# Constant matrices made by GpSimd instead of VectorE, and a newly searched order, in an attention and feed-forward kernel

## The chip, the cores and the metric

The kernel runs on one core of one Trainium2 chip. The metric is the device time of that core in microseconds, the median over the runs given. The core has a matrix engine (TensorE, PE in the profile; its weight loads are PEld), VectorE (DVE), ScalarE (ACT), GpSimd (POOL), and SyncE (SP), which here only issues transfers. Each engine works through its own list of instructions strictly in order, and waits at an instruction until the semaphores that it names have been raised.

## The reference, cut to what matters

Attention with a decay ("forgetting") runs over 8 batches of 8 heads, with 576 positions and a head size of 64. Its output, one row of 512 numbers per token, goes through a bilinear feed-forward layer.

```
scores = (q @ k.T) / 8
cum    = cumsum(log(clip(f, 1e-4, 1)))          # per head, along the sequence
scores = scores + cum[:, None] - cum[None, :]   # then -1e9 above the diagonal
attn   = softmax(scores)
x      = attn @ v                               # (4608 tokens, 512)
out    = ((x @ w_a) * (x @ w_b)) @ w_out        # 512 -> 1536 -> 512
```

## The kernel before, in words

**Work and tiles.** One batch has 8 heads, taken in pairs: pair t (0 to 31; t = 4 x batch + pair) is two heads. Two pairs make a unit u (0 to 15). The scores of a unit are made in four groups g: rows of positions 0 to 255, 256 to 383, 384 to 511, and 512 to 575. ScalarE takes the exponential ("exp0" to "exp4", by block of 128 rows), VectorE takes row maxima ("max") and reciprocals of the sums ("rec"), GpSimd multiplies by the reciprocals ("norm", line 567), and the normalized matrix is turned, on TensorE in batch 0 ("ptr", line 591, with an eviction "evp") and by transposing transfers (line 583) afterwards, so that TensorE can multiply it with v ("pv", "pve", "pv4", lines 611 to 636). The result, turned, lies in `xT` and is the input of the feed-forward layer.

The feed-forward layer runs over strips of tokens: 256 tokens from token 0, from 256 and from 512, 384 from 768, then strips of 512. For each of 12 column blocks fb, TensorE makes `psa` and `psb` (line 874, four matmuls each); one of them is copied to SBUF ("aev"), VectorE multiplies (line 890), and at the end `pso` (line 899) is made and stored. Weights `wa` and `wb` come in two pieces each: blocks fb 0 to 3 in one transfer ("the low piece", 512 KB in SBUF), blocks 4 to 11 in another ("the high piece", 1,024 KB). GpSimd's queue issues these transfers (line 365).

**Constants.** At the start, `constants` makes a 128x128 identity on GpSimd. From it VectorE makes `pick` and `eye` (reductions over blocks of the identity), `neg` (the identity times -60000), `sel` (which rows of the cumulative sum a matmul picks), `low` (ones below the diagonal, by blocks) and a row of ones `cw["1"]` for the scan. The first three batches add the decay and the mask by small matmuls with these matrices; `sel` is needed by "crep", which spreads the cumulative sum. GpSimd sets the padding (`paddings`) to zero.

**Order.** Nothing is scheduled when the kernel is built. Every step is an `op` with a number, and a table `ORDER` gives the sequence in which they are recorded; from it follows the order on each engine and the order in which buffers rotate. A second table `CHOICE` has one letter for each step that may run on more than one engine (A ScalarE, D VectorE, P GpSimd, S SyncE). Forty steps "fill" (line 178) are four matmuls each of the identity with itself, into a buffer that nobody reads: they only occupy TensorE.

## Time and profile before

| | before |
|---|---|
| runs | 401.02, 402.35, 398.56 us; median 401.02 |
| profiled execution, first to last instruction | 400.7 us |
| PE busy | 383.2 us (96%) |
| DVE busy | 315.3 us (79%) |
| ACT busy | 250.0 us (62%) |
| POOL busy | 253.6 us (63%) |
| granted TensorE clock, mean | 0.986 |

The profiled execution has only its span; no separate time is listed for it. The span is 0.3 us under the median of the three runs, and inside their spread. The page of the profile cuts the span in 40 slices of 10 us and gives for each the busy share in tenths; `PEclk` is the clock that TensorE was granted. A matmul counts as busy until its modelled end, so that a stretch in which PE is 95% busy can hold more idle time than 5%. From about 120 us on PE is busy without a gap; before that the four compute engines share the load.

### The profile page before, as it was taken

The page shows a single profiled execution, that of the slowest core. Times are in us where ns is not written, and L with a number is a line of the kernel's source. Part 1 is how long each engine was busy: PE and PEld are TensorE (multiplying, and loading weights), DVE is VectorE, ACT ScalarE, POOL GpSimd, SP SyncE. Part 2 cuts the span into 40 slices and gives each one's busy share as a digit, 9 for nine tenths or more (in the row PEclk, how much of TensorE's full clock was granted, in tenths as well). Part 3 has the DMA queues.
Part 4 walks back from the last instruction along what each step waited for, and adds up shares of the span by engine and source line. Part 5 has one row for each costly group of instructions (what it writes and reads, how often), then busy time and mean ns, then how long its engine had stood idle before and what let it go on. Part 6 is the DMA issues. An engine that isn't in the chain of part 4 may idle for free.

```text
span 400.7 us, 11076 instructions
## 1 busy us (share of the span) xinstructions
PE 383.2 (96%) x4040; PEld 212.0 (53%) x4040; DVE 315.3 (79%) x907; ACT 250.0 (62%) x757; POOL 253.6 (63%) x424
## 2 busy tenths in 40 slices
PE   8598799998999999999999999999999999999996
PEld 7466576765855544454445454544444444444553
DVE  8989798976778988997988889898969892373560
ACT  5798766666667778758785777577868673300011
POOL 3889876887397876897896849787968553000000
PEclk9889999998999999999999999999999999999999
DMA  7999989989999999999999999999997729000102
GB/s 282 240 186 289 204 177 224 213 150 215 208 301 208 227 171 330 201 277 212 295 187 286 211 255 273 233 241 190 276 187 218 157 66 202 28 2 36 71 0 79
DMA packets 148311, 78.22 MB, mean 195 GB/s; under 512 B 130592, under 2 KB 133408, under 8 KB 148256
## 3 DMA queue, kind: packets, MB, share of 16 engines
q1 hardware_dynamic: 144272, 72.53, 77.4%
q0 software_dynamic: 3696, 4.72, 7.0%
q8 instruction: 31, 0.51, 0.5%
q10 hardware_dynamic: 288, 0.26, 0.2%
q14 instruction: 24, 0.20, 0.1%
HBM read 49.69 MB, written 9.58 MB: 148 GB/s over the span
## 4 chain that ended last, share of the span: by engine, by line
PE 79%; DMA 9%; DVE 4%; POOL 2%; ACT 2%; issue 2%; SPq 0%; POOLq 0%; DVEq 0%; ACTq 0%
PE pso L899 22%; PE psa L874 22%; PE psb L874 21%; PE sc L401 8%; DMA wa<-in_moe_w_a_dram 5%; PE pv L611 2%; DVE st L488 2%; DMA k<-in_k_dram 1%; PE pv L613 1%; PE sc L636 1%; DMA PTB<-spread 1%; DMA PTB<-PB 1%; DVE qT L302 1%; PE pv L623 1%; ACT PB L550 1%
## 5 line engine op out<-in xcount | busy, mean ns | idle before, releaser
L874 PE MATMUL psa<-xT,wa 128*128 128x512 f16 (+2 forms) x528 | 116.2, 343 | 2.3 <-DMA wa<-in_moe_w_a_dram 1.7
L874 PE MATMUL psb<-xT,wb 128*128 128x512 f16 (+2 forms) x528 | 116.2, 343 | 0.1
L899 PE MATMUL pso<-wout,ht 128*128 128x512 f16 (+1 forms) x444 | 98.4, 374 | 0.0
L567 POOL TENSOR_SCALAR PA<-PA,st 128x128 f16<-128x128 f16 (+2 forms) x162 | 76.0, 482 | 31.8 <-DVE st L559 20.4
L890 DVE TENSOR_TENSOR ht<-psb,a 128x512 f16<-128x512 f32 (+2 forms) x132 | 76.2, 589 | 22.0 <-PE psb L874 15.0
L512 DVE CUSTOM_DVE_ANT_0 S<-sc,spread 128x128 f32<-128x128 f32 (+3 forms) x160 | 86.7, 567 | 7.7 <-PE sc L401 5.4
L138 ACT CAST a<-psa 128x512 f16<-128x512 f32 (+2 forms) x85 | 43.5, 515 | 55.9 <-PE psa L874 53.8
L874 PEld LDWEIGHTS <-wa 128*128 128x128 f16 x528 | 50.1, 99 | 45.5 <-issue 3.7
L874 PEld LDWEIGHTS <-wb 128*128 128x128 f16 x528 | 50.4, 99 | 41.5 <-issue 1.7
L567 POOL TENSOR_SCALAR PB<-PB,st 128x512 f16<-128x512 f16 (+1 forms) x84 | 58.7, 712 | 15.7 <-DVE st L559 14.6
L550 ACT ACTIVATE PA<-S,st 128x256 f16<-128x256 f32 (+2 forms) x120 | 59.9, 502 | 12.5 <-DVE st L512 12.4
L899 PEld LDWEIGHTS <-ht 128*128 128x128 f16 x444 | 41.7, 98 | 46.8 <-issue 1.3
L488 DVE TENSOR_REDUCE st<-sc 128x2 f32<-128x512 f32 (+7 forms) x68 | 46.3, 723 | 6.0 <-PE sc L401 5.3
L401 PE MATMUL sc<-kT,qT 32*128 32x128 f16 (+5 forms) x960 | 41.7, 272 | 5.5 <-ACT PA L550 2.1
L550 ACT ACTIVATE PB<-S,st 128x512 f16<-128x512 f32 x40 | 28.5, 714 | 7.9 <-DVE st L512 7.9
L401 PEld LDWEIGHTS <-qT 32*128 32x128 f16 (+1 forms) x960 | 18.6, 96 | 26.7 <-issue 14.4
L142 DVE CAST a<-psa 128x512 f16<-128x512 f32 (+2 forms) x47 | 26.2, 560 | 7.2 <-PE psa L874 6.6
L559 DVE RECIPROCAL st<-st 128x2 f32<-128x2 f32 x128 | 18.5, 157 | 14.0 <-ACT PA L550 8.7
L142 POOL CAST k<-k 128x1152 f16<-128x1152 f32 (+1 forms) x15 | 20.5, 1367 | 8.9 <-DMA k<-in_k_dram 8.9
L138 ACT COPY osb<-pso 128x512 f32<-128x512 f32 (+1 forms) x22 | 12.4, 570 | 19.9 <-PE pso L899 15.1
L138 ACT CAST xT<-pv 128x512 f16<-128x512 f32 (+2 forms) x39 | 17.0, 446 | 11.8 <-PE pv L636 5.8
L140 POOL TENSOR_SCALAR q<-q 128x1152 f16<-128x1152 f32 (+1 forms) x15 | 20.6, 1372 | 5.0 <-DMA q<-in_q_dram 4.2
(98 smaller groups left out, 491.5 us busy)
## 6 DMA issues: line engine op xcount, KB each, us to landing
spread<-cum_d SPq DMA_DIRECT2D x20, 576.0 KB, 5.9
out_dram<-osb SPq DMA_DIRECT2D x35, 256.0 KB, 3.8
q<-in_q_dram SPq DMA_DIRECT2D x15, 576.0 KB, 7.3
k<-in_k_dram SPq DMA_DIRECT2D x15, 576.0 KB, 5.2
v<-in_v_dram SPq DMA_DIRECT2D x32, 256.0 KB, 6.1
wout<-in_moe_w_out_dram POOLq DMA_DIRECT2D x3, 512.0 KB, 8.7
v<-in_v_dram SPq DMA_DIRECT2D x8, 128.0 KB, 7.2
wb<-in_moe_w_b_dram POOLq DMA_DIRECT2D x1, 1024.0 KB, 13.5
```

What stands on the lines that cost most here:

```text
L138: nc.scalar.copy(out=out_, in_=in_)
L140: ENG[e].tensor_scalar(out=out_, in0=in_, scalar1=0.125, scalar2=1.0, op0=MUL, op1=MUL)
L142: ENG[e].tensor_copy(out=out_, in_=in_)
L401: nc.tensor.matmul(out=dst, lhsT=lhsT, rhs=rhs, start=start, stop=stop, skip_group_check=True)
L488: nc.vector.tensor_reduce(out=m if i == 4 else st[:, 2 * i:2 * i + 2][:, h:h + 1] if isinstance(x, list) else m, in_=y, axis=AXX, op=MAX, ...
L512: nc.vector.tensor_tensor_reduce(out=o, in0=x, in1=y, scale=-1.0, scalar=3e38, op0=ADD, op1=MIN, accum_out=m)
L550: nc.scalar.activation(out=p_blocks(t, i)[:, :, h, :], in_=x.rearrange("p (j k) -> p j k", k=128), func=EXP, scale=sign, bias=st[:, c:c + ...
L559: nc.vector.reciprocal(out=st[:, 20 + 2 * i:22 + 2 * i], in_=st[:, 10 + 2 * i:12 + 2 * i])
L567: ENG[e].tensor_scalar(out=p, in0=p, scalar1=st[:, c:c + 1], scalar2=1.0, op0=MUL, op1=MUL)
L874: nc.tensor.matmul(out=o, lhsT=w16[:, db, 128 * fb:128 * fb + 128], rhs=tokens(db, t0, n), start=(db == 0), stop=(db == 3))
L890: nc.vector.tensor_tensor(out=ht[:, 0:n], in0=T.pop(("psb", t0, fb))[:, 0:n], in1=T.pop(("a16", t0, fb))[:, 0:n], op=MUL)
L899: nc.tensor.matmul(out=o, lhsT=T[("ht", t0, fb)][:, 128 * tb:128 * tb + 128], rhs=wout16[:, fb, c], start=(fb == 0), stop=(fb == 11))
```

## The change

Three things change. First, `pick`, `eye`, `neg`, `sel`, `low` and the ones are made by GpSimd. The two reductions are replaced by three additions that fold the identity (64, 32, 16 columns) through a new small tile `half`. Second, `low` keeps only its last two steps on VectorE (a scan and a subtraction); the zeros and ones of it are a GpSimd step of its own. Third, `ORDER` and `CHOICE` are other tables, found by a new search in which transfers land late at random; every engine's order differs.

```diff
+    half = fixed("half", [128, 64])
...
+    def low_blocks(_):
+        nc.gpsimd.memset(low, 0.0)
+        for a in range(1, 4):
+            nc.gpsimd.memset(low[:, a, 0:32 * a], 1.0)
+
     def lows(_):
-        nc.vector.memset(low, 0.0)
-        for a in range(1, 4):
-            nc.vector.memset(low[:, a, 0:32 * a], 1.0)
         nc.vector.tensor_tensor_scan(out=step, data0=cw["1"][:, 0:32], data1=eye, initial=0.0, op0=MUL, op1=ADD)
...
     def picks(_):
-        with nc.allow_low_precision("ones and zeros"):
-            nc.vector.tensor_reduce(out=pick, in_=ident.rearrange("p (a r) -> p r a", r=16), axis=AXX, op=ADD)
-            nc.vector.tensor_reduce(out=eye, in_=ident.rearrange("p (a n) -> p n a", n=32), axis=AXX, op=ADD)
-        nc.vector.tensor_scalar(out=neg, in0=eye, scalar1=NEGBIG, scalar2=1.0, op0=MUL, op1=MUL)
-        nc.vector.memset(sel, 0.0)
+        nc.gpsimd.tensor_tensor(out=half, in0=ident[:, 0:64], in1=ident[:, 64:128], op=ADD)
+        nc.gpsimd.tensor_tensor(out=eye, in0=half[:, 0:32], in1=half[:, 32:64], op=ADD)
+        nc.gpsimd.tensor_tensor(out=pick, in0=eye[:, 0:16], in1=eye[:, 16:32], op=ADD)
+        nc.gpsimd.tensor_scalar(out=neg, in0=eye, scalar1=NEGBIG, scalar2=1.0, op0=MUL, op1=MUL)
+
+    def selections(_):
+        nc.gpsimd.memset(sel, 0.0)
         for c in range(SETS):
             for e in range(2):
-                nc.vector.tensor_copy(out=sel[:, c, e].rearrange("p (g e r) -> p g e r", e=2, r=16)[:, :, e],
+                nc.gpsimd.tensor_copy(out=sel[:, c, e].rearrange("p (g e r) -> p g e r", e=2, r=16)[:, :, e],
...
-    o_pick = op("D", "pick", picks, [o_id])
+    o_pick = op("P", "pick", picks, [o_id])
+    o_sel = op("P", "sel", selections, [o_pick])
+    o_lowm = op("P", "lowm", low_blocks)
...
     def f_ones(_):
-        nc.vector.memset(warm, 1.0)
-        nc.vector.memset(cw["1"], 1.0)
+        nc.gpsimd.memset(warm, 1.0)
+        nc.gpsimd.memset(cw["1"], 1.0)
...
-    o0 = op("D", "ones", f_ones)
+    o0 = op("P", "ones", f_ones)
...
-            bm = op("E", "crep", lambda _, n=n, a=a: rows_mm(n, *a), [o4, o5, o_pick], hi - lo)
+            bm = op("E", "crep", lambda _, n=n, a=a: rows_mm(n, *a), [o4, o5, o_sel], hi - lo)
...
-    o_low = op("D", "low", lows, [o0, o_pick])
+    o_low = op("D", "low", lows, [o0, o_pick, o_lowm])
...
     CHOICE = """
-        DPAADDAAPPAPAAPADPADDAAADADDDDDAADDDDAAADAAADDAAAADAAAAADAAAAAAADAAAAAADDAAADADADDAAAAAADDAAAAAAAAA
...
+        DPADAPADDPAPAPPAAPPDAADDAADAAADDDDDDAAADDDAAADDDADAAAAADDDDADAAAAAAAAADAADADAAAADDAAAAAADDAAAAADAAA
...
```

What the tables move is shown at three places. The first is VectorE's list at the start of the program, before the change. `cum_f` holds f and the row of ones, `xT_68` holds `sel` and `xT_66` holds `low`; L206 clips f, L213 is the scan.

```order
L198 MEMSET warm 128x1
L199 MEMSET cum_f 128x576
L160 TENSOR_REDUCE pick<-ident 128x16
L161 TENSOR_REDUCE eye<-ident 128x32
L162 TENSOR_SCALAR neg<-eye 128x32
L163 MEMSET xT_68 32x256
L166 COPY xT_68<-eye 32x4x16 x4
L150 MEMSET xT_66 128x256
L152 MEMSET xT_66 128x32
L152 MEMSET xT_66 128x64
L152 MEMSET xT_66 128x96
L153 SCALAR_TENSOR_TENSOR step<-cum_f,eye 128x32
```

The same place after the change (the last of the padding, then f, the scan, and the first two transposes of q and k, L309):

```order
L178 MEMSET nv_74 64x256
L178 MEMSET nv_75 64x256
L213 TENSOR_SCALAR cum_f<-cum_f 64x320
L213 TENSOR_SCALAR cum_f<-cum_f 64x256
L220 SCALAR_TENSOR_TENSOR cum_f<-cum_f,cum_l 64x256
L143 CAST wout_73<-cum_f 32x256
L220 SCALAR_TENSOR_TENSOR cum_f<-cum_f,cum_l 64x320
L156 SCALAR_TENSOR_TENSOR step<-cum_f,eye 128x32
L158 TENSOR_SCALAR xT_67<-step 128x4x32
L309 STREAM_TRANSPOSE qT<-q_218 128x9x64
L309 STREAM_TRANSPOSE kT<-k_229 128x9x64
```

VectorE's constants are gone and the padding stands in their place. One of two casts and the subtraction that follow the scan before (L142 and L220 there) have left VectorE: the cast for ScalarE, both subtractions are now on GpSimd. Between there and the fifth column block of the first strip, VectorE also loses the cast of a part of q (L140, 128x512), three evictions net of transposed blocks, one of a `pv`, and five reciprocals, which stand later or on ScalarE; it gains two evictions of the spread cumulative sum and one more "aev".

The second place is GpSimd's list where the weights are issued, before the change. `wa_70` and `wb_71` 128x4x512 are the low pieces, 128x4x1024 the high ones; L567 is the normalization, L142 a cast of v.

```order
L142 CAST nv_73<-v_355 128x1024
L567 TENSOR_SCALAR PA<-PA,st 128x128 x2
L567 TENSOR_SCALAR PA<-PA,st 128x2x128 x2
L365 DMA wa_70<-in_moe_w_a_dram 128x4x512
L567 TENSOR_SCALAR PA<-PA,st 128x2x128 x2
L365 DMA wb_71<-in_moe_w_b_dram 128x4x512
L567 TENSOR_SCALAR PA<-PA,st 128x128
L142 CAST nv_74<-v_377 128x1024
L567 TENSOR_SCALAR spread_80<-spread_80,st 128x2x128
L365 DMA wb_71<-in_moe_w_b_dram 128x4x1024
L365 DMA wa_70<-in_moe_w_a_dram 128x4x1024
```

The same after the change: three of the four weight transfers, and then, 17 rows further on, the fourth.

```order
L143 CAST k_310<-wout_73 128x512
L372 DMA wb_72<-in_moe_w_b_dram 128x4x512
L141 TENSOR_SCALAR q_435<-q_300 128x1152
L143 CAST nv_74<-v_302 128x1024
L372 DMA wa_71<-in_moe_w_a_dram 128x4x512
L574 TENSOR_SCALAR PA<-PA,st 128x128
L372 DMA wa_71<-in_moe_w_a_dram 128x4x1024
L143 CAST k_461<-k_345 128x1152
```

```order
L574 TENSOR_SCALAR PA<-PA,st 128x2x128
L574 TENSOR_SCALAR PA<-PA,st 128x128
L574 TENSOR_SCALAR PA<-PA,st 128x3x128
L574 TENSOR_SCALAR PB_77<-PB_77,st 128x4x128 x2
L372 DMA wb_72<-in_moe_w_b_dram 128x4x1024
L574 TENSOR_SCALAR PB_78<-PB_78,st 128x4x128
```

The low pieces and the high piece of `wa` are issued before almost all normalizations. The high piece of `wb` stands behind fifteen normalizations of the first two row blocks, one of a third and the two of pair 0's fourth row block (PB_77, 128x4x128).

The third place is TensorE in the strip from token 768, behind `psa` of its third column block. Before the change the scores of unit 6 follow (L401):

```order
L874 LDWEIGHTS wa_70
L874 MATMUL psa<-xT_68,wa_70 128x384
L874 LDWEIGHTS wa_70
L874 MATMUL psa<-xT_69,wa_70 128x384
L401 LDWEIGHTS qT
L401 MATMUL sc_2880<-kT,qT 128x128
```

After it, two fills follow (L183), eight matmuls of which the first is shown:

```order
L881 LDWEIGHTS wa_71
L881 MATMUL psa<-xT_69,wa_71 128x384
L881 LDWEIGHTS wa_71
L881 MATMUL psa<-xT_70,wa_71 128x384
L183 LDWEIGHTS ident
L183 MATMUL idle<-ident 128x128
```

All in all 40 fills are there in both. Before the change 20 of them stand ahead of the first scores and 20 between there and the strip from token 512, none later. After it 13 stand ahead of the first scores, 17 from there to the strip from 512, 2 in that strip, and 8 in the strip from token 768 and behind it. Of the rest of TensorE's list, the fifth column block of the first strip (`psa` and `psb`, fb 4) is reached after 11 fills, 25 transposing matmuls (the second parts of pairs 0 and 2, and two of pairs 0 and 1) and one `pve` (14 matmuls) less than before. In the strip from token 512, `pve` of pair 7 (rows 256 to 511) and `pv4` of pair 7, which stood ahead of its first block, now stand behind 13 of its blocks. The scores of group 2 of unit 5, which stood ahead of the strip from token 768, now stand behind its first block.

102 lines of the change are left out of this document (64 added, 38 removed), and 108 rows, old and new, of the table ORDER.

## The prediction

> **What bounds the kernel now.** I read the busy table, then TensorE's clock, then the busy time of the engines in stretches, then what TensorE waited for, and last the order of time at the places that the change touches.
>
> ```profile
> PE 383.2 (96%) x4040; PEld 212.0 (53%) x4040; DVE 315.3 (79%) x907; ACT 250.0 (62%) x757; POOL 253.6 (63%) x424
> PEclk9889999998999999999999999999999999999999
> ```
>
> The view of stretches has the engines' busy time after each stretch's length, in the order PE, PEld, DVE, ACT, POOL, then the clock, the DMA share and GB/s. I cut it at TensorE's milestones: first scores (10.79), `psb` of the fifth block of the first strip (44.66), strip from token 512 (95.58), strip from token 768 (119.79). I call these stretches A, B, C and D.
>
> ```profile
> 10.79:44.66 33.87, 25.30 (x483) 19.21 (x483) 30.72 (x76) 26.95 (x97) 29.90 (x49) 0.90 1.08 234
> 44.66:95.58 50.92, 48.28 (x824) 34.24 (x822) 44.09 (x98) 34.22 (x114) 40.20 (x66) 1.00 1.02 193
> 95.58:119.79 24.21, 23.76 (x348) 16.57 (x345) 16.12 (x38) 15.33 (x53) 14.28 (x24) 0.93 1.08 246
> 119.79:397.30 277.51, 277.46 (x2309) 134.58 (x2307) 215.34 (x671) 166.52 (x485) 164.77 (x274) 1.00 0.78 184
> ```
>
> ```profile
> PE sc L401 <- ACT PA L550: 2.1, 1, 2.1
> PE sc L401 <- DVE st L559: 2.1, 1, 2.1
> PE pv L636 <- DMA PTB<-spread: 1.8, 1, 1.8
> PE psa L874 <- DMA wa<-in_moe_w_a_dram: 1.7, 1, 1.7
> ```
>
> In A, VectorE is busy 30.72 of 33.87 us (91%) and TensorE 75%: VectorE sets the pace. In B, TensorE is at 95%. In D it is idle 0.05 us in 277.5, so what is added to its list there is paid in full, and what VectorE saves there buys nothing. The four longest waits all lie ahead of D. So the change can win only in the first 120 us; what it wins there moves all of D forward.
>
> **The constants.** The start, in order of time:
>
> ```profile
> 0.73 0.59 SPq L195 DMA_DIRECT2D cum_f<-in_f_dram  x1
> cum_f<-in_f_dram SPq DMA_DIRECT2D x1, 144.0 KB, 2.7
> 0.80:3.76 2.96, 2.40 (x23) 2.40 (x24) 2.69 (x17) 1.42 (x2) 0.43 (x2) 1.00 0.54 154
> 3.76 0.51 DVE L206 TENSOR_SCALAR cum_f<-cum_f 64x320 f32<-64x320 f32 x2
> 5.54 0.86 POOL L140 TENSOR_SCALAR q<-q 128x640 f16<-128x640 f32 x1 [4.23 <-DMA q<-in_q_dram]
> 7.28 0.92 POOL L142 CAST k<-k 128x640 f16<-128x640 f32 x1 [0.89 <-DMA k<-in_k_dram]
> 7.52 1.03 DVE L220 TENSOR_TENSOR wout<-cum_f,wout 32x320 f16<-32x320 f32 x1
> 8.18 0.91 POOL L220 TENSOR_TENSOR wout<-cum_f,wout 32x256 f16<-32x256 f32 x1
> 8.48 1.20 DVE L302 STREAM_TRANSPOSE qT<-q 128x576 f32<-128x576 f32 x1
> 10.79 0.40 PE L401 MATMUL sc<-kT,qT 32*128 32x256 f16 x8 [0.47 <-DVE kT L302]
> ```
>
> VectorE's 2.69 us of constants end at 3.76, where the clipping of f begins. f itself has landed at 0.73 + 2.7 = 3.43. So taking the constants off VectorE lets f's chain start only 0.33 us earlier; the rest was hidden by the load of f. The padding that VectorE gets lies in the same gap: on GpSimd its larger half took 0.99 us for two tiles, below.
>
> GpSimd sat idle 4.23 us before its first cast at 5.54, since q had not landed. Into this gap go fifteen instructions. The nearest rows of GpSimd:
>
> ```profile
> 11.05 0.99 POOL L173 MEMSET nv<- 64x512 f16 x2
> 19.81 0.38 POOL L567 TENSOR_SCALAR PA<-PA,st 128x128 f16<-128x128 f16 x1
> ```
>
> Three memsets of about 512 columns at 0.50 us are 1.5 us; the other twelve, all of 128 columns or fewer, cost at most 0.38 each, 4.6 us, and at least the half of that, 2.3. From 1.31 us, where the identity is done (5.54 less 4.23), they end between 5.1 and 7.4; I take 6.0, nearer the low end because most have 16 to 64 columns. The q cast then ends at 6.9 instead of 6.4, the subtraction for the first 256 columns at 7.8, the cast of k at 8.7. VectorE, without the second subtraction (1.03 us), is ready for the transpose of q at 8.48 - 1.03 - 0.33 = 7.1 and for that of k at 8.3. So k's cast is late by 0.4 us in this sum, by 1.8 at the high end and by nothing at the low one. First scores: 10.79 - 1.36 + 0.4 = 9.8.
>
> **Stretch A: VectorE.** Up to the multiplication of the fifth block, VectorE's list loses work and gains some. The rows that price it:
>
> ```profile
> 12.65 1.16 DVE L140 TENSOR_SCALAR q<-wout 128x512 f16<-128x512 f32 x1
> L142 DVE COPY xT<-psP 128x768 f16<-128x768 f16 x7 | 3.7, 546 | 0.0
> L142 DVE CAST xT<-pv 128x256 f16<-128x256 f32 x6 | 2.4, 408 | 0.0
> L559 DVE RECIPROCAL st<-st 128x2 f32<-128x2 f32 x44 | 6.0, 154 | 2.4 <-ACT PA L550 2.3
> ```
>
> Lost: the subtraction 1.03, the q cast 1.16, three evictions at 0.55 (1.64), one of `pv` 0.41, a small cast of about 0.25, five reciprocals at 0.15 (0.77): 5.3 us. Gained: two evictions and one "aev" of like size, 3 x 0.41 = 1.2. Net 4.1, and 0.3 from the earlier f: 4.4 us. The bounds: 5.8 if VectorE's idle 3.2 us shrink too by half, 2.0 if the moved work only makes it wait for ScalarE, which gets the q cast and one more eviction.
>
> What TensorE needs there besides is the high piece of `wb`.
>
> ```profile
> 22.51 0.75 POOL L365 DMA_DIRECT2D wa<-in_moe_w_a_dram  x1
> wb<-in_moe_w_b_dram POOLq DMA_DIRECT2D x1, 1024.0 KB, 13.5
> wa<-in_moe_w_a_dram POOLq DMA_DIRECT2D x1, 1024.0 KB, 21.7
> wb<-in_moe_w_b_dram POOLq DMA_DIRECT2D x1, 512.0 KB, 8.8
> 31.81 0.69 POOL L567 TENSOR_SCALAR PB<-PB,st 128x512 f16<-128x512 f16 x1
> 44.21 0.61 PE L874 MATMUL psa<-xT,wa 128*128 128x256 f16 x4 [1.65 <-DMA wa<-in_moe_w_a_dram]
> 44.66 0.60 PE L874 MATMUL psb<-xT,wb 128*128 128x256 f16 x4
> ```
>
> Before, `wa`'s high piece, last in the queue, landed at 22.51 + 21.7 = 44.2 and held TensorE for 1.65 us. After, `wb`'s is last, issued behind pair 0's normalizations, the second of which ran at 31.81 before. With VectorE 4 us ahead I put the issue at 28.5. Its landing takes between 8.8 us (the half as large piece) and 13.5 us (the same piece, which then still had two ahead of it): 37.3 to 42.0, middle 39.7. VectorE would allow `psb` at 44.66 - 4.4 = 40.3. So I take **A: -4.4**, with little to spare.
>
> **Stretch B.** TensorE now has behind that point what stood ahead of it: 25 transposes and 14 `pv` matmuls, and a fill more on balance; `pv4` and the second `pve` of pair 7 leave for C. The view of time around the strip from 512:
>
> ```profile
> 91.59 0.61 PE L401 MATMUL sc<-kT,qT 32*128 32x512 f16 x8
> 92.25 0.26 PE L401 MATMUL sc<-neg,xT 32*128 32x32 f16 x16
> 94.28 0.35 PE L636 MATMUL pv<-PTB,nv 128*64 128x64 f16 x10 [1.77 <-DMA PTB<-spread]
> 95.12 0.62 PE L178 MATMUL idle<-ident 128*128 128x128 f16 x8
> 95.58 0.93 PE L874 MATMUL psa<-xT,wa 128*128 128x256 f16 x4
> 97.15 1.06 PE L874 MATMUL psa<-xT,wa 128*128 128x256 f16 x4
> 98.00 1.06 PE L874 MATMUL psb<-xT,wb 128*128 128x256 f16 x4
> ```
>
> A fill is half of 95.12 to 95.58, 0.23 us, so a transpose of the same 128 columns is 0.058. `pv4` and `pve` of pair 7 fill 94.28 to 95.12, 0.84. In: 25 x 0.058 + 0.65 + 0.23 = 2.3. Out: 0.84. The wait of 1.77 for pair 7's turned block goes whole: 13 blocks of 0.45 (44.21 to 44.66) stand ahead of it now, 5.8 us, more than three times the wait. **B: -0.3**; +1.5 if a like wait comes for another pair.
>
> **Stretch C.** Behind that wait the clock fell: from 95.58 a block of four matmuls takes 0.85 (97.15 to 98.00) against 0.45, and C's mean is 0.93. 0.07 x 24.21 = 1.7 us. If the wait goes I let this go too. In come pair 7's 0.84 and two fills (0.46), out go the scores of a group 2, 91.59 to about 92.5, 0.9. **C: -1.3**; +0.4 if the clock falls all the same.
>
> The Trainium skill, page TensorE: Matmul & The Clock Gate, Part 1: The HAM clock gate, has the clock halve after an idle window of about 3.4 us, watched in free-running windows. The trace agrees only in part: here the half clock followed a wait of 1.77 us, with work on both sides of it. By the page's length alone that wait is not the cause, C would be +0.4, and the sum 399.4 instead of 397.7.
>
> **Stretch D.** Eight fills at 0.23 and the 0.9 of that group are new, and nothing is idle to take them: **D: +2.7**; +0.9 if the fills fall where the new order makes TensorE wait anyway.
>
> Sum: -4.4 - 0.3 - 1.3 + 2.7 = -3.3. On the span of 400.7 that is 397.4, and with the 0.3 us by which the median of the runs lies above the span, **397.7 us**.
>
> **Rivals.**
>
> *The last weights come too late (slower).* Place: `psb` of the fifth block of the first strip. TensorE's list is in order, and the rest of that strip, the transposes of batch 0 and the scores of unit 2's later groups are all queued behind it; VectorE and ScalarE then wait for TensorE. If GpSimd comes to the issue no earlier than 32.5 (31.81 + 0.69) and the landing takes 13.5 to 21.7, `psb` starts at 46.0 to 54.2. A is then +1.3 to +9.5, middle +5.4; B, C and D sum to +1.1; 400.7 + 6.5 + 0.3 = **407.5**. It decides from a landing at 47.6: there the total is +4.0, 1%. For it speaks that this transfer is alone behind eighteen normalizations; against it, that the three ahead of it are issued several us earlier and leave the queue free.
>
> *The lead is lost in B (no change).* B is 95% TensorE, so VectorE's lead may find TensorE unable to follow. Then only the first scores (-1.0) and C are won: -1.0 - 0.3 - 1.3 + 2.7 = +0.1, **401.1**. The 2.1 us waits for VectorE's and ScalarE's results in A speak against it.
>
> *More is won.* A at its bound, another 1 us of waits gone in B, and D's fills under waits: -5.8 - 1.3 - 1.3 + 0.9 = -7.5, **393.5**. For it: A held both waits of 2.1 us and the 1.65 us for the weights; against it: D has had no waits to hide a fill under.
>
> *The cold clock stays (no change).* The clock also falls between 10 and 30 us (8 in two slices), where TensorE waits 2.1 us twice. If it falls by a share of idle time over a longer stretch, and not by the one wait, the fewer fills ahead of the first scores and the moved work leave it as low: C is +0.4, **399.4**. Against it: between 30 and 90 us, with short waits alone, it never fell. That is also what the page's rule in stretch C would make of the time.
>
> **How the numbers follow.** About 1%, 4.0 us, is what a measurement of this kernel tells from no change: faster means under 397.0. The forecast (its own range 395 to 400.5) gets 0.45, of which 0.25 is under 397.0. More won 0.13; cold clock 0.07; lead lost 0.20; late weights 0.15, nearly all over 405. Faster 0.25 + 0.13 = 0.38; slower 0.15; same 0.47. The range: the low end adds up the low bounds, -5.8 - 1.3 - 1.3 + 0.9 = -7.5, and leaves half a chance in ten under it: 393.0. The high end takes A at -2.0, B and C at +1.5 and +0.4, D at 2.7, +2.6, that is 403.6, and leaves out the late weights.
>
> **What would show it.** Right: first scores near 9.8; the fifth `psb` near 40.3 with no wait for `wb` over 1 us; strip 512 near 90.9; no clock under 1.0 around it; `psa` of the strip from 768 near 113.8; and then D longer by 2 to 3 us. Wrong: a wait of TensorE for `wb` of several us before 50; a wait of `pv` for a turned block of another pair; a new gap in D; or GpSimd over 90% busy up to 45 us with its constants ending past 7.

## The result and the profile after

| | before | after |
|---|---|---|
| median of 16 runs each, same chip | 401.76 us (398.56 to 404.19) | 405.56 us (403.57 to 408.50) |
| after / before | | 1.0098, 95% interval 1.0077 to 1.0119 |
| profiled execution, first to last instruction | 400.7 us | 402.5 us (that run took 404.24 us) |

The changed kernel is 1.0% slower: 3.8 us in the medians, 1.8 us in the two profiled executions. The forecast was 397.7 us; the range ended at 403.6. A run's time is 1.7 to 1.8 us longer than its span wherever both are listed, so the profiled execution of before, with its span of 400.7, is one of about 402.5 us, some 0.7 above the median.

The busy table and TensorE's clock from the page of the changed kernel:

```profile
PE 384.1 (95%) x4040; PEld 211.5 (53%) x4040; DVE 314.8 (78%) x909; ACT 247.9 (62%) x746; POOL 257.3 (64%) x434
PEclk9869999999999999999999999999999999999999
```

Hardly a number of it differs from before. The view of stretches, cut at the same four milestones of TensorE as in the prediction (columns as there):

```profile
10.78:41.18 30.40, 24.70 (x430) 17.24 (x430) 27.23 (x64) 24.82 (x88) 26.31 (x42) 0.83 1.10 229
41.18:93.03 51.85, 49.86 (x840) 35.61 (x841) 45.85 (x113) 36.04 (x116) 42.95 (x67) 1.00 0.96 209
93.03:115.47 22.44, 22.18 (x349) 16.51 (x348) 16.46 (x42) 13.11 (x47) 13.28 (x23) 1.00 1.10 241
115.47:399.20 283.73, 282.20 (x2369) 137.53 (x2367) 218.17 (x675) 167.01 (x488) 166.32 (x280) 1.00 0.73 182
```

A is 3.5 us shorter than before and C 1.8; B is 0.9 longer and D 6.2 (283.73 against 277.51). D's idle time on TensorE is now 1.53 us, not 0.05. The half clock around 96 us is gone (C's clock is 1.00, it was 0.93); A's clock fell from 0.90 to 0.83.

Where the time of D goes is seen best at places up to which both lists have done the same TensorE work. I count the matmuls in the list ahead of a place, by shape. Ahead of the strip from 768 the new list has eight fills fewer (1.8 us) and one group of scores (0.85 us: 117.20 to 118.05 in before, 116.87 to 117.72 after); ahead of the strip from 2176, that from 3200 and the last one the counts are equal.

| start of TensorE's work on | before | after | difference |
|---|---|---|---|
| strip from 768 | 119.79 | 115.47 | -4.32, of which 2.7 is work put off (the prediction's own price for it) |
| strip from 2176 | 226.44 | 226.50 | +0.06 |
| strip from 3200 | 304.99 | 306.90 | +1.91 |
| last strip | 373.80 | 375.72 | +1.92 |

So the true lead at 115 us is 1.6 us. By 226 us nothing is left of it, and another 1.85 us is lost between 226 and 307: **D loses 3.5 us beyond what was put into it.** The largest single piece lies at 282 us. The changed kernel in order of time there, TensorE's scores (L408) and VectorE's decayed scores (L519), which free the scores' buffer in PSUM (the rows of `pv`, 281.41 to 282.64, are left out):

```profile
280.34 1.20 DVE L309 STREAM_TRANSPOSE kT<-k 128x576 f32<-128x576 f32 x1
280.82 0.66 PE L408 MATMUL sc<-kT,qT 32*128 32x128 f16 x16
281.48 0.56 DVE L519 CUSTOM_DVE_ANT_0 S<-sc,spread 128x384 f32<-128x384 f32 x1
281.96 0.55 DVE L519 CUSTOM_DVE_ANT_0 S<-sc,spread 128x384 f32<-128x384 f32 x1
282.44 0.55 DVE L519 CUSTOM_DVE_ANT_0 S<-sc,spread 128x384 f32<-128x384 f32 x1
282.64 0.40 PE L408 MATMUL sc<-kT,qT 32*64 32x512 f16 x2
282.92 0.55 DVE L519 CUSTOM_DVE_ANT_0 S<-sc,spread 128x384 f32<-128x384 f32 x1
283.53 0.68 PE L408 MATMUL sc<-kT,qT 32*64 32x512 f16 x14 [0.49 <-DVE st L519]
```

And before:

```profile
278.42 1.21 DVE L302 STREAM_TRANSPOSE kT<-k 128x576 f32<-128x576 f32 x1
279.15 0.51 PE L401 MATMUL sc<-kT,qT 32*128 32x128 f16 x16
279.59 1.04 PE L874 MATMUL psb<-xT,wb 128*128 128x512 f16 x4
279.69 0.56 DVE L512 CUSTOM_DVE_ANT_0 S<-sc,spread 128x384 f32<-128x384 f32 x1
280.46 1.03 PE L874 MATMUL psa<-xT,wa 128*128 128x512 f16 x4
281.19 0.55 DVE L512 CUSTOM_DVE_ANT_0 S<-sc,spread 128x384 f32<-128x384 f32 x1
282.10 0.69 PE L401 MATMUL sc<-kT,qT 32*64 32x512 f16 x16
```

Both show the second and third group of scores of pairs 26 and 27 (unit 13). Before, two feed-forward groups (`psb`, `psa`) and a `pv` stand between the two, 2.5 us from 279.59 to 282.10, and the third group runs through in one piece of sixteen. After, only two `pv` stand there, 1.2 us from 281.41 to 282.64: the first two matmuls of the third group start at 282.64, the other fourteen 0.89 us later, when VectorE has read the scores ahead of them. The page counts 0.40 us of these 0.89 as busy and 0.49 as idle; a share of TensorE's waits in D is inside its busy time.

At the start, the constants on GpSimd and VectorE's list beside them, in the changed kernel:

```profile
3.65 1.35 POOL L171 COPY xT<-eye 32x64 f16<-32x64 f16 x4
5.52 0.32 POOL L153 MEMSET xT<- 128x32 f16 x3
5.93 0.86 POOL L141 TENSOR_SCALAR q<-q 128x640 f16<-128x640 f32 x1
6.14 0.79 DVE L143 CAST wout<-cum_f 32x256 f16<-32x256 f32 x1
8.47 1.21 DVE L309 STREAM_TRANSPOSE qT<-q 128x576 f32<-128x576 f32 x1
8.60 0.73 ACT L139 CAST k<-k 128x512 f16<-128x512 f32 x1 [0.39 <-DMA k<-in_k_dram]
10.78 0.40 PE L408 MATMUL sc<-kT,qT 32*128 32x256 f16 x8 [2.29 <-DVE kT L309]
```

GpSimd is done with the constants at 5.84 (forecast 6.0). The first scores start at 10.78, not at 9.8: k was in SBUF, and its cast could start, only at 8.60, and VectorE came to the transpose of q only at 8.47, where the prediction had it ready at 7.1. The cast of k before:

```profile
7.25 0.73 ACT L138 CAST k<-k 128x512 f16<-128x512 f32 x1 [0.22 <-DMA k<-in_k_dram]
```

### The profile page after: what moved, and what is told of

Same layout as the page of the kernel before. It is cut to its first block, busy times and chain, and to the rows that moved or that the text cites. A ratio compares the mean times of both kernels' runs of the same rounds, so it can differ in the third digit from the quotient of the medians.

```text
span 402.5 us, 11035 instructions
## 1 busy us (share of the span) xinstructions
PE 384.1 (95%) x4040; PEld 211.5 (53%) x4040; DVE 314.8 (78%) x909; ACT 247.9 (62%) x746; POOL 257.3 (64%) x434
## 4 chain that ended last, share of the span: by engine, by line
PE 42%; DVE 7%; issue 1%; DMA 0%; ACT 0%; DVEq 0%; ACTq 0%
PE pso L906 13%; PE psa L881 12%; PE psb L881 12%; DVE S L519 4%; PE sc L408 3%; PE pv L618 1%; DVE ht L897 1%; PE pv L620 1%; DVE a L143 1%; DVE qT L309 1%; PE sc L643 1%; DMA out_dram<-osb 0%; DVE kT L309 0%; ACT osb L139 0%; DVE xT L143 0%
## 5 line engine op out<-in xcount | busy, mean ns | idle before, releaser
L574 POOL TENSOR_SCALAR PA<-PA,st 128x256 f16<-128x256 f16 (+2 forms) x162 | 75.2, 478 | 41.4 <-issue 22.6
L519 DVE CUSTOM_DVE_ANT_0 S<-sc,spread 128x128 f32<-128x128 f32 (+3 forms) x160 | 87.1, 568 | 4.5 <-PE sc L408 2.7
L139 ACT CAST a<-psa 128x512 f16<-128x512 f32 (+2 forms) x78 | 40.9, 524 | 50.7 <-PE psa L881 47.6
L906 PEld LDWEIGHTS <-ht 128*128 128x128 f16 x444 | 41.7, 98 | 47.0 <-issue 1.5
L495 DVE TENSOR_REDUCE st<-sc 128x2 f32<-128x512 f32 (+8 forms) x68 | 46.5, 724 | 8.0 <-PE sc L408 4.4
L408 PE MATMUL sc<-kT,qT 32*128 32x128 f16 (+5 forms) x960 | 42.9, 270 | 7.3 <-DVE kT L309 2.3
L143 DVE CAST a<-psa 128x256 f16<-128x256 f32 (+2 forms) x54 | 29.2, 545 | 8.4 <-PE psa L881 8.1
L408 PEld LDWEIGHTS <-qT 32*128 32x128 f16 (+1 forms) x960 | 18.9, 95 | 29.7 <-issue 15.2
L557 ACT ACTIVATE PA<-sc,st 128x256 f16<-128x256 f32 (+2 forms) x42 | 19.6, 482 | 8.2 <-DVE st L495 6.1
L574 POOL TENSOR_SCALAR spread<-spread,st 128x256 f16<-128x256 f16 (+4 forms) x36 | 19.6, 552 | 6.2 <-DVE st L566 4.0
L139 ACT CAST xT<-pv 128x512 f16<-128x512 f32 (+2 forms) x32 | 14.9, 470 | 13.9 <-PE pv L620 7.1
```

The lines of the kernel that those rows point to most:

```text
L139: nc.scalar.copy(out=out_, in_=in_)
L143: ENG[e].tensor_copy(out=out_, in_=in_)
L408: nc.tensor.matmul(out=dst, lhsT=lhsT, rhs=rhs, start=start, stop=stop, skip_group_check=True)
L495: nc.vector.tensor_reduce(out=m if i == 4 else st[:, 2 * i:2 * i + 2][:, h:h + 1] if isinstance(x, list) else m, in_=y, axis=AXX, op=MAX, ...
L519: nc.vector.tensor_tensor_reduce(out=o, in0=x, in1=y, scale=-1.0, scalar=3e38, op0=ADD, op1=MIN, accum_out=m)
L557: nc.scalar.activation(out=p_blocks(t, i)[:, :, h, :], in_=x.rearrange("p (j k) -> p j k", k=128), func=EXP, scale=sign, bias=st[:, c:c + ...
```

## The experiments

Each ratio is to runs of the kernel before on the same chip. The changed kernel itself is at 1.0098.

### One part of the change alone

**Constants on GpSimd, old order.** The functions and dependencies of the changed kernel, the old `ORDER` and `CHOICE` (new steps behind `pick`).

```diff
     ORDER = """
-        (new table)
+        (table of before; sel and lowm behind pick)
```

> The constants made by GpSimd, with the sequence and the engine letters of the kernel before. Theory (the loss lies in the new order behind 119 us): nothing is lost, 401.3 to 402.3 against a kernel before at 401.8; the first scores stay near 10.8, since k lands late enough to hide GpSimd's constants. Rival (the constants cost it, by GpSimd's slower instructions and by VectorE being slowed beside them): 403.5 to 405.5, with first scores 1 us or more later.

401.51 us, ratio 1.0006 (0.9982 to 1.0029). Who makes the constants is worth nothing in the time, either way. At the start it did cost something, which the theory did not have:

```profile
5.03 0.40 DVE L158 TENSOR_SCALAR xT<-step 128x128 f16<-128x128 f16 x1 [2.20 <-POOL xT L151]
```

VectorE waited 2.20 us for GpSimd's part of `low` and then clipped f at 5.13, where before did so at 3.76. The first scores started 1.3 us later (12.11, as the rival had it) and the strip from 768 0.8 later, but from the strip from 2688 on only 0.06 were left: the old order took up this late start.

**New order up to the strip from 768, the old one behind; and the reverse.**

```diff
     ORDER = """
-        (new table)
+        (new table up to psa of strip 768, block 0; then what is left, in the order of before; 8 fills in front)
```

> The new sequence and letters up to the strip from token 768, then what is left in the old sequence with the old letters; the 8 fills left over stand before the first scores. Theory (the head is won, the tail loses): the strip from 768 starts 4 us earlier than before, and from there the time runs as before, 397.3 to 398.7. Rival (the lead is work put off, which any tail must pay): 400.5 to 402.5. Rival (the constants cost it): 403 or more.

```diff
     ORDER = """
-        (new table)
+        (table of before up to psa of strip 768, block 0; then what is left, in the new order)
```

> The old sequence up to the strip from token 768, with the constants on GpSimd, then the new sequence and letters. All 40 fills are in the head here. Theory (the new tail loses about 4 us by scores that wait for VectorE, besides 1.8 by its fills, which are not in this kernel): 405 to 407. Rival (the tail costs only its fills and the group of scores that it took over): 401.5 to 402.5.

The first: 404.41 us, 1.0089 (1.0054 to 1.0124), a miss. The joint, the place where one table follows the other, cost 5.8 us between the strips from 768 and from 1152 (117.6 to 151.6 us in this run); behind it the old tail lost 0.3, but it did not take up the delay either: 3.6 us late at the strip from 1152, 3.9 at the end. TensorE's two longest waits behind the joint, in order of time:

```profile
121.03 0.81 PE L881 MATMUL psb<-xT,wb 128*128 128x384 f16 x4 [1.30 <-ACT osb L139]
132.55 0.44 PE L643 MATMUL sc<-PTB,nv 128*64 128x64 f16 x10 [1.78 <-DMA PTB<-PB]
```

ScalarE's evictions and a turned block of the probabilities were not as far as the old tail assumes, and the clock halved once (132.6 to 136.0).

The second: 406.32 us, 1.0119 (1.0081 to 1.0157), as expected: with no lead to spend and no fills, the new tail lost 4.7 us between the strip from 768 and the end. A joint stands in this run too, but 2.3 of the 4.7 us go far behind it, between the strips from 2688 and from 3200 (41.00 us, before 38.71), and the changed kernel takes the same 41.00 there. So D's own order loses, whatever stands ahead of it.

The traces of other runs show the same. From the strip from 768 to that from 2176 the changed kernel takes 111.03 us, before 106.65. Four more runs below have its lists unchanged up to there (TensorE's old list from 2176, the old order from 2176, and the two with one place widened): they reach the strip from 768 anywhere from 115.06 to 116.32 and take 111.01 to 111.04. An early start is carried on whole, then; it is the stretch that is longer.

**The eight late fills moved ahead of the first scores**, else the new order.

```diff
-  8 fills among the scores and feed-forward of strips 768 to 2176
+  2 fills ahead of the first crep, 6 ahead of the first scores
```

> The new order, but the 8 fills that stood in the strip from 768 and behind it now stand before the first scores. Theory (TensorE has no time there, so each is paid): 1.5 to 2 us under the new kernel, 403.6 to 404.1. Rival (they stand where TensorE waits for VectorE anyhow): 405 to 406, no change from the new kernel at 405.6.

404.85 us, 1.0082 (1.0051 to 1.0112): 0.7 us gained, not 1.8, and the interval alone would allow both nothing and 1.8. The profiled execution says more: from the strip from 768 to the end of TensorE's work it took 284.5 us without a fill, the changed kernel 283.8 with eight; against before it lost 6.9 us there. So the fills stood under waits; D was not longer by them. And the 0.7 us fits the granted clock of the runs: of the changed kernel's 16 runs, 11 have 0.979 (median 405.89 us) and 3 have 0.987 (404.24). With the fills early 5 of 9 have 0.987, and their median is 404.18: the same at the same clock.

### Which list loses the time in D

**The engines of the evictions as before** (70 steps from the strip from 768 on).

```diff
     CHOICE = """
-        (new letters)
+        (new letters up to strip 768, then those of before)
```

> The changed kernel in its new order, but from strip 768 on the 70 evictions that the search gave to another engine (21 of `aev` to VectorE and 19 from it, and some of `ev4` and `ocopy`) are with the engine they had before. Theory, that D loses time through the places of VectorE's decayed scores in its list and not through its share of the evictions: no real difference, 405.0 to 406.2 us (the changed kernel has 405.56). Rival, that the evictions newly on VectorE make the scores wait: some 2 to 4 us come back, 401.6 to 403.6.

410.23 us, 1.0187 (1.0147 to 1.0228): outside both expectations, 3.6 us slower than the changed kernel by the ratios. New order and new letters fit each other.

**TensorE's list as before from the strip from 2176.**

```diff
-  TensorE, from strip 2176: new list
+  TensorE, from strip 2176: list of before (87 operations at another place); VectorE, ScalarE, GpSimd, SyncE: new lists
```

> The changed kernel, but TensorE's list from strip 2176 on is that of the kernel before (87 of its operations stand at another place); the lists of the other engines stay new. Between 280 and 350 us the changed kernel's TensorE stands 2.4 us longer than that of before. Theory, that VectorE's list makes those waits: they stay, 404.8 to 406.5 us. Rival, that TensorE asks for its scores too early or in the wrong order: about 2.4 us come back, 402.8 to 403.6.

424.79 us, 1.0541 (1.0497 to 1.0585), worse than either expected. TensorE then waited 5.2 us for VectorE's products, 4.3 for its decayed scores and 6.0 for copies on both engines. It tells little of the cause, only how tightly the lists are tied.

**92 decayed scores one place earlier in VectorE's list.**

```diff
-  VectorE:  mul  dec
+  VectorE:  dec  mul      (also past ocopy, tqk, aev; 92 dec, strip 768 to the end)
```

Here `dec` is a decayed score, `mul` a product, `ocopy` an output copy, `tqk` a turned q or k.

> The changed kernel, but in VectorE's list 92 of the decayed scores behind the start of strip 768 stand one place earlier, ahead of 28 products, 5 output copies, 4 turned q or k and 3 evictions; no other engine's list changes. Theory, that scores wait because the decays that free their buffer stand behind such work: the nine waits of 0.2 to 0.9 us in D shrink by some half to all of their 4 us, and the products pay back under 1: 402.0 to 404.5 us. Rival, that VectorE's pace as a whole or the softmax behind it sets the scores: 405.2 to 406.5, and the waits only move.

412.68 us, 1.0243 (1.0200 to 1.0287). The theory of that run falls. What TensorE waited for in it, behind 120 us:

```profile
PE pso L906 <- DVE ht L897: 2.2, 3, 1.3
PE sc L408 <- DVE st L519: 1.2, 3, 0.5
PE psb L881 <- DVE ht L897: 0.9, 2, 0.7
```

The scores' waits stay, and the products (`ht`) that had to stand back by one are now waited for as well.

**The old order from the strip from 2176 on.**

```diff
     ORDER = """
-        (new table)
+        (new table up to psa of strip 2176, block 0; then what is left, with order and letters of before)
```

> The changed kernel up to the first matmul of strip 2176, and from there the order and the engines of before for all that is left. Of the two stretches in which the changed kernel's TensorE stands longer than that of before, 120 to 200 us (1.5 us) stays and 280 to 350 us (2.4 us) goes. Theory, that the loss is made where the new order stands: 402.6 to 403.8 us. Rival, that attention comes late out of the earlier part and the old order then waits for it at once: 405 to 407.

407.80 us, 1.0118 (1.0065 to 1.0170): the rival. 3.1 us went in the 40 us behind the joint (waits of 1.2 us for ScalarE and 1.1 for a turned block), none behind it. The old tail is good only behind the old head.

### Is it VectorE's, or ScalarE's, pace?

**Half of each product left out from the strip from 768 on**, in the changed kernel and in the one before. Half the hidden values are missing; TensorE's work is the same.

```diff
-        nc.vector.tensor_tensor(out=ht[:, 0:n], in0=T.pop(("psb", t0, fb))[:, 0:n],
-                                in1=T.pop(("a16", t0, fb))[:, 0:n], op=MUL)
+        m = 256 if t0 >= 768 else n
+        nc.vector.tensor_tensor(out=ht[:, 0:m], in0=T.pop(("psb", t0, fb))[:, 0:m],
+                                in1=T.pop(("a16", t0, fb))[:, 0:m], op=MUL)
...
+        tb = tb % 2 if t0 >= 768 else tb
```

> The changed kernel with half the product from strip 768 on: VectorE multiplies only the first 256 columns of each of the 96 products there, and the output matmuls read these columns twice, so that TensorE's work stays the same; half the hidden values are left out. It takes some 0.25 us from each product, 24 us of VectorE's time, without a change of any list. Theory, that VectorE's pace is what makes the scores wait in the changed order's D: what it lost there against before, 3.5 us, goes, and its lead at 120 us, 1.5, shows: from 1 us below to 1.5 above before's time with the same cut. Rival, that the lists wait for something else (ScalarE, a turned block's transfer): it stays 3 to 5 us above before's time with the same cut.

> The kernel before with the same half of the product left out from strip 768 on. Both theories: TensorE stays the bound, 0 to 3 us below before, since its scores wait little for VectorE.

After: 403.66 us, 1.0054 (1.0019 to 1.0090); before: 401.55, 0.9992 (0.9961 to 1.0023). Between both: 2.1 us, where it was 3.8; neither the theory (at most 1.5) nor the rival (3 to 5). In the profiled execution the cut shortened the changed kernel's way from the strip from 768 to the last one by 0.65 us. The view of stretches from 280 to 350 us, first of the changed kernel without the cut:

```profile
280.00:350.00 70.00, 69.26 (x598) 32.65 (x597) 52.19 (x167) 43.39 (x123) 41.12 (x74) 1.00 0.66 168
```

The changed kernel with the cut:

```profile
280.00:350.00 70.00, 69.36 (x599) 32.66 (x597) 47.53 (x168) 43.38 (x123) 41.12 (x74) 1.00 0.70 174
```

And the kernel before, without the cut:

```profile
280.00:350.00 70.00, 70.00 (x579) 32.57 (x578) 50.26 (x164) 44.68 (x125) 39.59 (x70) 1.00 0.72 165
```

By the cut VectorE (third busy time) lost 4.7 us of work there, but TensorE's idle time only went from 0.74 to 0.64, where before has none. The third group of scores in unit 13 still stood 0.89 us. VectorE's load alone is not what D lost.

**Half of each `aev` copy left out**, in the same two kernels; the product reads the copied columns twice, so the other half's values are missing.

```diff
-        cast(e, a16[:, 0:n], T.pop(("psa", t0, fb))[:, 0:n])
+        m = n // 2 if t0 >= 768 else n
+        cast(e, a16[:, 0:m], T.pop(("psa", t0, fb))[:, 0:m])
...      (the product takes a16[:, 0:m] twice)
```

> The changed kernel with half of each eviction of the first half of the feed-forward left out from strip 768 on: 256 of 512 columns are copied (by ScalarE or VectorE, as the order says), and the product reads them twice; the values of the other half are left out. ScalarE loses the most by it. Theory, VectorE's pace: it has only a third of these copies, so a part of the 3.5 us goes: 1 to 3.5 us above before's time with the same cut. Rival, ScalarE's evictions come late in the changed order: at most 1 above before's time with the same cut.

> The kernel before with the same half of the evictions left out. Both theories: 0 to 2 us below before.

After: 404.88 us, 1.0075 (1.0046 to 1.0104); before: 403.74, 1.0033 (1.0001 to 1.0065). Before did not become faster by it, which neither side expected and which I can't explain; that it became slower is hardly more than the interval. The times, 1.1 us apart, are too uncertain to tell the theories apart, but the profiled execution of the changed kernel is clear: between 125 and 390 us the cut took 10.8 us of work from ScalarE and 5.9 from VectorE, and from the strip from 768 to the last one it lost 6.2 us against before, as without the cut. What these copies load on either engine is not what D lost.

### The distance between two groups of scores

In these cuts `qk0` to `qk3` are the four groups of scores of a unit, `psa`, `psb` and `pso` matmuls of the feed-forward layer, `pv` and `pv4` those with v. Where an expectation below says pair 6, 8, 9, 12 or 13, or pairs 11 to 15, it means the units of these numbers. Its distances, 1.8 us and 0.2, count too little: the rows above show 2.5 and 1.2 us of other matmuls between the second and third group.

**Widened at one place of the changed kernel** (unit 13, TensorE's list alone).

```diff
-  psb fb6, psa fb7, pv4, pv4, qk1, pv, pv, qk3
+  pv4, pv4, pv, qk1, psb fb6, psa fb7, pv, qk3
```

> The changed kernel, but in TensorE's list at one place the eight operations around the second and third group of scores of pair 13 stand as in the kernel before: two feed-forward groups of 0.86 us each lie between them again (1.8 us of other matmuls, not 0.2). No other list changes. Theory, that the distance between groups of scores in TensorE's list makes the stalls: at that place 0.88 us of the third group, 0.35 in front of the second and 0.49 of the fourth go, 1.7 us in all: 403.6 to 404.2 us against 405.56. Rival, that VectorE comes to these scores late whatever stands between: 405.0 to 406.

405.47 us, 1.0076 (1.0050 to 1.0101), the rival's time. In the profiled executions TensorE ends 0.5 us earlier than in the changed kernel, but 0.4 of this was there at the strip from 768 already, far ahead of the edit; the place itself gave 0.1, not 1.7. The third group, in order of time:

```profile
279.18 0.68 DVE L143 CAST a<-psa 128x512 f16<-128x512 f32 x1
279.91 1.20 DVE L309 STREAM_TRANSPOSE kT<-k 128x576 f32<-128x576 f32 x1
280.96 0.53 DVE L519 CUSTOM_DVE_ANT_0 S<-sc,spread 128x384 f32<-128x384 f32 x1
282.04 0.40 PE L408 MATMUL sc<-kT,qT 32*64 32x512 f16 x2
283.00 0.68 PE L408 MATMUL sc<-kT,qT 32*64 32x512 f16 x14 [0.56 <-DVE st L519]
```

It still stands 0.95 us: VectorE has a copy of `psa` and the transpose of k ahead of the decayed scores, and comes to them at 280.96.

**Five groups of scores later** (the one above and four single moves).

```diff
-  qk1(u6), psb | qk0(u8), psb | qk2(u9), psa | pv4, pv4, qk1(u12), pv, pso, pv, qk3, pso
+  psb, qk1(u6) | psb, qk0(u8) | psa, qk2(u9) | pv4, pv4, pv, qk1(u12), pso, pv, pso, qk3
```

> The one above, and at four more places (the second group of pairs 6 and 12, the first of pair 8, the fourth of pair 9) a group of scores stands one feed-forward group later in TensorE's list. In the changed kernel these stall 0.37, 0.36, 0.48 and 0.24 us more than in before. Theory: another 1 to 1.5 us go, 402.2 to 403.2 us. Rival, that at these the decays are late for another reason: as the one above, or slower.

406.16 us, 1.0103 (1.0066 to 1.0141): no gain, the rival. The moved groups became shorter from start to end as expected (0.75 to 0.38, 0.83 to 0.35, 0.96 to 0.51 us), but in unit 6 the next group grew from 0.57 to 1.04.

**Narrowed at five places of the kernel before** (units 11 to 15, old order).

```diff
-  pv4, pv4, pv, qk1, psb, psa, pv, qk3
+  psb, psa, pv4, pv4, qk1, pv, pv, qk3      (at units 12 and 14 two pso instead of psb, psa)
```

> The order of the kernel before (with GpSimd's constants, which cost nothing there: 401.5 us), but for the pairs 11 to 15 the two feed-forward groups that lie between the second and third group of scores stand ahead of the second, as the changed kernel has it for pair 13. Theory: each of the five costs 0.9 to 1.7 us: 406 to 410 us. Rival: within 1 us of 401.5.

409.64 us, 1.0181 (1.0140 to 1.0222), against 1.0006 for the same order with the wide places: **7 to 8 us for five places, 1.5 each**, as expected. TensorE between 200 and 350 us:

```profile
200.00:280.00 80.00, 78.21 (x656) 36.48 (x654) 66.98 (x222) 54.51 (x165) 58.70 (x97) 1.00 0.93 228
280.00:350.00 70.00, 67.51 (x582) 32.41 (x581) 48.05 (x160) 43.86 (x125) 39.50 (x70) 1.00 0.68 164
```

Its idle time is 4.3 us where before it had 0.05, and the largest wait is the same: six times the scores (`sc`) for VectorE's `st`, 2.6 us. So a list can lose this much by the place of two feed-forward groups, with no work added. But the wait does not always fall on the third group: at unit 13, the place at 282 us, that group ran through in one piece here, and a `pv` ahead of it waited 0.68 us for ScalarE.

**The five groups later, and the fills early.**

```diff
+  the five moves above
+  8 late fills ahead of the first scores
```

> The second run, with the 8 late idle matmuls of 0.23 us moved ahead of the first scores. In the changed order alone that gave 0.7 us, since without them the scores waited in their place. Theory: with the places widened more of their 1.8 us comes out, 0.7 to 1.8 below the second run: 400.5 to 402.5 us. Rival, that they stand under waits still: at most 0.3 below the second run.

405.08 us, 1.0067 (1.0040 to 1.0094): 1.1 us below the run of the five moves, inside what was expected of the step, but not in the expected place.

**The one place wide, and VectorE's two copies there on ScalarE.**

```diff
-  aev fb5, aev fb6 of strip 2688: VectorE
+  aev fb5, aev fb6 of strip 2688: ScalarE
```

> The run with one place widened, and the two evictions of 0.66 and 0.68 us that stand on VectorE ahead of the decays there (feed-forward groups 5 and 6 of strip 2688) given to ScalarE, as in the kernel before. Theory, that distance and VectorE's work in it have to go together: the third group's stall falls from 1.52 to about 0.6 us, and the time by 0.9 to 1.4 from that run: ratio to before 1.004 to 1.006. Rival, that ScalarE now comes late with the two and TensorE's matmuls wait for a free buffer instead: no gain, 1.007 to 1.010.

406.20 us, 1.0084 (1.0059 to 1.0109): the rival. The third group now runs through in one piece:

```profile
280.39 0.62 PE L408 MATMUL sc<-kT,qT 32*128 32x128 f16 x16 [0.67 <-ACT xT L139]
283.44 0.69 PE L408 MATMUL sc<-kT,qT 32*64 32x512 f16 x16
287.79 1.02 PE L881 MATMUL psa<-xT,wa 128*128 128x512 f16 x4 [0.72 <-DVE ht L897]
```

Its stall is gone as forecast (from 1.52 us for the group to 0.57), and two new ones of like size stand around it: the second group waits for ScalarE, which has the two copies now, and a feed-forward group for a product. From the strip from 2688 to that from 3200 this run took 41.7 us, the changed kernel 41.0.

**All of it together.**

```diff
+  the one place wide, its two copies on ScalarE, qk0(u8) and qk2(u9) later, pv ahead of qk1(u12)
+  8 late fills ahead of the first scores
```

> The run above, with the first scores of pair 8 and the fourth of pair 9 one feed-forward group later (these shrank their stall from 0.83 to 0.35 and from 0.96 to 0.51 us), the second of pair 12 behind an attention product, and the 8 late idle matmuls ahead of the first scores. Theory: 1 to 2.5 us below the run above: ratio to before 0.999 to 1.003. Rival, that what is moved comes back at the next group of scores: within 0.5 us of the run above.

404.73 us, 1.0071 (1.0038 to 1.0103): 1.5 us below the run before it in the medians, inside what was expected of the step and about the gain of the fills and their clock, but above the expected ratio; no closer to the kernel before than 0.4% at the low end. No version beat the kernel before.

## Why the prediction was wrong

**First scores at 9.8: wrong, 10.78.** The step priced GpSimd's constants nearly right (5.84, forecast 6.0), but it had two things wrong. VectorE was to be ready for the transpose of q at 7.1 and came to it at 8.47: `low`'s scan and subtraction, which stood ahead of f before, now stand behind f's chain (7.65 to 8.47), and beside GpSimd's work the two clips took 1.06 us in place of 0.51 and the cast 0.79 in place of 0.28. And k's landing was taken as fixed, but it varies with one and the same list: in the three profiled executions with before's start, ScalarE's cast of k began at 7.25, 8.51 and 8.97, and the first scores at 10.79, 11.05 and 11.50. In the changed kernel it began at 8.60; both reasons ended together there. That the constants cost nothing in total is shown by the run that has them alone (1.0006).

**A, -4.4: nearly right, -3.5.** The fifth `psb` started at 41.18, forecast 40.3. VectorE's list in A is shorter by 3.5 us of busy time (27.23 against 30.72). The wait for `wb` is there, and at this place it is the rest:

```profile
41.18 0.61 PE L881 MATMUL psb<-xT,wb 128*128 128x256 f16 x4 [0.92 <-DMA wb<-in_moe_w_b_dram]
```

The transfer was issued at 29.5 (the prediction put it at 28.5) and took 11.7 us (between its bounds of 8.8 and 13.5), so it landed 1.5 us behind the middle that I took. It set little: in the run with one place widened, whose lists are the same up to here, `wb` was there in time and the fifth `psb` started at 40.03, but that of the next block then waited 1.49 us for VectorE's product and started at 42.55; in the changed kernel it started at 42.63. So VectorE sets the pace here, as the step had it. The rival of the late weights, which needed 47.6, was far off.

**B, -0.3: wrong, +0.9.** The wait for pair 7's turned block went, as forecast. But at 80 us a wait came that the step did not have, for VectorE's products, and at 76 one of 0.3 us for ScalarE; together they are the difference of 1.2 us.

```profile
PE psb L881 <- DVE ht L897: 0.9, 1, 0.9
```

**C, -1.3: right, -1.8.** The half clock around 96 us went. The stretch was cold with the wait of 1.77 us ahead of it and warm without. Other runs fit: waits of TensorE of 2.10 us (before with half of each `aev`, at 93 us) and 1.78 us (old tail behind the new head, at 131) were followed by 3.4 us of half clock as well, waits of 0.89, 0.94 and 1.66 us between 86 and 95 us of runs with the old head were not. The Trainium skill, page TensorE: Matmul & The Clock Gate, Part 1, asks for an idle window of about 3.4 us; the traces do not bear out that length, and the rival built on it did not come.

**D, +2.7: wrong in kind, +6.2.** This is the step that failed. It said that TensorE is idle for 0.05 us in D, that its list sets the end, and that what is added is paid in full; so it put the new order's own waits in D at nothing. Four things in the runs go against that. The fills were free: without them the time at the same clock is the same (404.18 and 404.24), and D is no shorter. The stretch from 768 to 2176 takes 4.4 us more in the new order whatever the start, where 2.65 of work were added. In the old order, which has as little idle time, a start 0.8 us late was taken up (the run with the constants alone), though one of 3.6 us was not (the old tail behind the new head). And five places narrowed cost 8 us with no work added. All four fit an end of D that is set by a loop over engines, in which TensorE makes scores, VectorE reads them and frees their buffer, and ScalarE and VectorE empty the feed-forward's buffers; that it is this loop is argued, not shown step by step. The busy time on the page hid the waits: at 282 us nearly half of a stall counted as busy.

What D lost beyond the work put off is 6.2 - 2.7 = 3.5 us: 1.6 of lead up to 226 us and 1.85 between 226 and 307. Since the fills only filled waits, the new order's own loss is larger than that: in the run with the fills early D lost 6.9 us, of which only the 0.85 of the group of scores is work put off. It is not the load of VectorE or ScalarE: half of each `aev` copy left out gave nothing in D, half of each product 0.65 us. The second part lies at 282 us and around it; such places have a price (1.5 us each where they were made on purpose), but undoing this one did not give the time back: widening it gave 0.1 us, and with VectorE relieved too the waits moved to ScalarE's evictions and VectorE's products. The loss belongs to the new order of all lists together. Which part of that order a search would have to change stays open, and so does the first part.

**The head's clock: not in the prediction.** The difference of the medians, 3.8 us, is 2.0 more than that of the two profiled executions. Some 0.7 of it is that the profiled execution of before lies above its median. The rest, 1.3, is that the profiled one of the changed kernel had a granted clock of 0.987, as only 3 of its 16 runs; 11 had 0.979 and took 1.65 us longer. In the profiled executions of the new order with 0.978 or 0.979 the additional half clock lies ahead of 31 us. Runs of the new list with the eight fills ahead of the first scores had 0.986 or 0.987 in 17 of 33 cases, those of the new list and its one-place variants without in 6 of 39. So moving idle matmuls out of the start costs clock there in most runs; the prediction gave the clock only to C.

**The rivals.** The nearest was the lost lead, 401.1 us, given 0.20; the lead was lost, but in D and not in B, and D took more than it. That C came out near its forecast and A within 0.9 us did not help the sum. The rival on the slow side named the wrong place. The sign "a new gap in D" was the one that came true.

## What to carry to other kernels

When a list runs at 95% or more on one engine, its busy time does not show that this engine sets the pace: look at the distance between two uses of the same buffer on it, and at whether pieces of one group (two matmuls, then fourteen) stand apart. Count a lead only between places at which both versions have done the same work, and compare the length of a stretch over several executions: one that is longer by the same amount, early start or late, loses by its own lists. A tuned order is one object over all engines: of twelve edits that gave the new order part of the old one or moved single steps in it, none came back to the old time, and the worst cost 4% more.

## What the runs showed of the hardware that was not expected

**VectorE and GpSimd hold each other up on small operations in SBUF.** The groups of VectorE's instructions in the first 9 us, after (columns: count, busy us, mean ns):

```profile
L213 DVE TENSOR_SCALAR cum_f<-cum_f 64x320 f32<-64x320 f32 (+1 forms) x2 | 1.1, 568 | 1.9 <-DMA cum_f<-in_f_dram 1.9
L143 DVE CAST wout<-cum_f 32x256 f16<-32x256 f32 x1 | 0.8, 790 | 0.0
L156 DVE TENSOR_TENSOR_SCAN step<-cum_f,eye 128x32 f16<-128x32 f16 x1 | 0.6, 612 | 0.0
```

And before:

```profile
L206 DVE TENSOR_SCALAR cum_f<-cum_f 64x320 f32<-64x320 f32 (+1 forms) x2 | 0.5, 295 | 0.0
L142 DVE CAST wout<-cum_f 32x256 f16<-32x256 f32 (+1 forms) x2 | 0.5, 282 | 0.0
L153 DVE TENSOR_TENSOR_SCAN step<-cum_f,eye 128x32 f16<-128x32 f16 x1 | 0.2, 160 | 0.0
```

Clip, cast and scan take 1.9, 2.8 and 3.8 times as long beside GpSimd's work. In two runs with the same lists at the start, the one held up was the one that came second. In the changed kernel GpSimd's cast of q began 0.21 us ahead of VectorE's cast (5.93 and 6.14, above). In the run with 92 decayed scores moved VectorE's cast began 0.10 us ahead:

```profile
5.82 0.28 DVE L143 CAST wout<-cum_f 32x256 f16<-32x256 f32 x1
5.92 1.64 POOL L141 TENSOR_SCALAR q<-q 128x640 f16<-128x640 f32 x1
```

Here VectorE's cast took 0.28 us and GpSimd's 1.64, where the changed kernel has 0.79 and 0.86. The Trainium skill, page SBUF — State Buffer, section Who interferes with whom, says that casts and `tensor_scalar` in some modes take an exclusive lock on ports shared with GpSimd, and that issue order decides who is blocked; these rows agree. It goes the other way too. GpSimd's four copies for `sel` took 1.35 us in the changed kernel, beside VectorE's clip of f, and 0.75 in the run with the constants alone, where VectorE stood waiting:

```profile
3.78 0.75 POOL L171 COPY xT<-eye 32x64 f16<-32x64 f16 x4
```

VectorE itself took 0.42 us for the four before.
